# Three quarters of a load on half of the DMA engines: two tilted 512 KB loads and an earlier loop on VectorE

## The chip, the cores and the metric

The kernel runs on one core of a Trainium2 chip. The metric is the device time of one execution in microseconds (us); of several runs the median is given. A core has a matrix engine (TensorE, PE in the profile; PEld is its weight load), VectorE (DVE), ScalarE (ACT), GpSimd (POOL) and SyncE (SP). SP issues all the loads here, and sixteen DMA engines carry them from HBM to SBUF.

## The reference

Two layers of one decode step: four tokens (B = 4, one position each, D = 512), each layer a grouped-query attention over a cache of 8192 positions and a gated feed-forward block. Both layers use the same weights and the same caches.

```
B, D, Hq, Hkv, Sk, Dh, F = 4, 512, 32, 8, 8192, 128, 1792        # bf16
def attention(x):
    q = (x @ wq).reshape(B, 1, Hq, Dh) transposed to heads
    scores = q . k_cache * Dh**-0.5          # each of 8 cache heads serves 4 query heads
    o = softmax(scores) @ v_cache
    return o.reshape(B, 1, Hq * Dh) @ wo
def ffn(x): return (silu(x @ w_gate) * (x @ w_up)) @ w_down
for layer in (1, 2):
    x = x + attention(layernorm(x))
    x = x + ffn(layernorm(x))
```

k_cache and v_cache are [4, 8, 8192, 128], so each is 64 MB. They have to be read once per layer, apart from what is kept on the chip between the layers.

## The kernel before

**Units.** A unit is one pair of token and cache head: 32 per layer. Its K tile and its V tile are 2 MB each, 128 partitions by 16 KB. SBUF has eight slots for such tiles (`kvf`, seen as `kv`), and the weights of the feed-forward block lie in two of the slots while they are needed. Three units of layer 1 stay in SBUF and are used first in layer 2.

**The order of the loads** is one list, `items`: K and V tiles of the units, the four pieces of `wo` (1 MB each, two DMAs of 512 KB) among the first of them, and `w_gate`, `w_up` and `w_down` at the end of a layer. `pump()` walks this list while the program is built and issues the next load when its slot is free; on the chip SP waits on semaphores for the engines that used the slot before. A load is described by `runs()`: 512 KB become 32 rows of 16 KB in HBM against 128 partitions by 4 KB in SBUF, and 2 MB become 64 rows of 32 KB. Some units are loaded in quarters of 512 KB (`part`); among them is the first K tile of layer 2 that isn't kept. Its first three quarters are issued in `ffn` of layer 1, after the products with `w_gate`, as `part(ks[0], NKEEP, 0, w6, sem_p[0])`, since they go to where `w_gate` lay.

**The work of a unit.** VectorE transposes the K tile in eight pieces (`turn`), TensorE multiplies them by the query (`scores`), VectorE takes the maximum, ScalarE the exponentials, VectorE transposes the probabilities (`turn_p`), TensorE multiplies them by V, and VectorE adds the parts up (`own_others`). After every fourth unit all four tokens of a cache head are done, and `out_proj` multiplies by a slice of `wo`: TensorE spreads the result, VectorE copies it to `o4` (that copy waits until all of `wo` is there), TensorE multiplies. Every TensorE, VectorE and ScalarE operation is recorded on a tape first, with the waits that it needs.

**The repeated blocks.** `roll()` plays the tape of each engine. It looks for the longest stretch of a layer in which four units (`CYCLE`) do the same as the next four, with the same semaphores in the waits, and emits that stretch as a loop; what lies ahead of it, between the layers and behind it is emitted unrolled. A wait inside the loop is on a value computed in a register, as the counts rise by a fixed step per turn. On VectorE the first `out_proj` has four waits more than the others (one for each piece of `wo`), so the loop of layer 1 starts at unit 7 of 32 and turns six times. TensorE's loop of layer 1, which has no such difference, starts at unit 3 and turns seven times.

**The semaphores.** A DMA raises its semaphore by 16 when it is complete, and the trace shows these increments one by one, as each DMA engine finishes its share. The four pieces of `wo` have a semaphore each.

In the profile nearly all operations of TensorE stand under line 99, those of VectorE and ScalarE under line 117, and the loads under line 135, as helpers emit them; waits of SP stand under line 79. The loops are at lines 885 to 891.

Of the kernel before, what the change touches and what calls it, by code (L numbers as in the profile page):

```python
# [27 lines left out]
class _Sync:  # L28
# [81 lines left out]
            if sig:  # L110
                ins.then_inc(self.prog[engname], 1)

    def op(self, engname, fn, reads=(), writes=(), sig=True):
        left = self._open(engname, self._need(reads, writes))
        if engname in self.LATE:
            name, args, kw = fn(_Call())
            self.tape[engname].append((repr((name, args, kw)), lambda e, _: getattr(e, name)(*args, **kw), left, sig, None))  # L117
        else:
            for sem, val in left:
                self.eng[engname].wait_ge(sem, val)  # L120
            ins = fn(self.eng[engname])
            if sig:
                ins.then_inc(self.prog[engname], 1)
        self.count[engname] += sig
        self._record(engname, (self.prog[engname], self.count[engname] + (not sig)), reads, writes)
# [20 lines left out]
def bass_interleave_layers__gqa_block_cached__swiglu_ffn__decode_kernel(  # L146
# [18 lines left out]
    P = 128  # L165
    assert Dh == P and B * Hq == P and D % P == 0 and F % P == 0 and B == 4
    KT = D // P
    FO = F // P
# [12 lines left out]
    NKEEP = 6  # L181
# [9 lines left out]
    with ExitStack() as es:  # L191
# [9 lines left out]
        kv = kvf[:, 0:NSLOT * SL].rearrange("p (s w) -> p s w", s=NSLOT)  # L201
# [15 lines left out]
        wo_sb = sb("wo_sb", [P, G, REP, D], BF16)  # L217
# [9 lines left out]
        o4 = sb("o4", [P, REP, B], BF16)  # L227
# [8 lines left out]
        pb = sb("pb", [P, SW], BF16)  # L236
# [8 lines left out]
        n = 2 * FO * B  # L245
# [13 lines left out]
        def few(ap):  # L259
# [6 lines left out]
        STEP, TOT, OUTB, LNB = 4, 5, 6, 7  # L266
# [7 lines left out]
        sem_p = [sem(f"sem_p{i}") for i in range(6)]  # L274
        sem_x = sem("sem_x")
        sem_w = {n: [sem(f"sem_{n}{i}") for i in range(c)]
                 for n, c in (("wq", KT), ("wo", 4), ("wg", KT), ("wu", KT), ("wd", FO // 2))}
        sem_out = sem("sem_out")
        es.enter_context(nc.Block())
        T = _Sync(nc, engines, prog)  # L280
# [6 lines left out]
             reads=["ident"], writes=["ident"])  # L287
        T.op("pool", lambda e: e.memset(quad[:], 0.0), writes=["quad"])
        for a in range(NA):
# [8 lines left out]
             reads=["ident"], writes=["head"])  # L298
        T.op("dve", lambda e: e.tensor_reduce(acc[:, 0:QB], identf[:].rearrange("p (y h) -> p y h", h=REP), AX.X, ALU.max),
             reads=["ident"], writes=["acc"])  # L300
        T.op("dve", lambda e: e.tensor_reduce(own[:], acc[:, 0:QB].rearrange("p (a y) -> p y a", a=NA)[:, 0:NV, :],
                                              AX.X, ALU.max),
             reads=["acc"], writes=["own"])
# [26 lines left out]
        for L in range(2):  # L330
            seq = [it for it in work(L) if it not in kept]
            for k, v in ((29, 27), (30, 28)):

                it = ("K", L, unit_order[L][k])
# [26 lines left out]
        def runs(src):  # L361

            n = src.shape[0] * src.shape[1] * 2
            return src.rearrange("(r k) n -> r (k n)", r=32 * -(-n // (32 * RUN)))

        def load_weight(name, i=0):
            if name == "wq":
                T.dma("sp", [(wq_sb[:, i, :], runs(A_wq[i * P:(i + 1) * P, :]))], sem_w["wq"][i], writes=[f"wq{i}"])
            elif name == "wo":
                n = G // 4  # L370
                w = REP * Dh
                T.dma("sp", [(wo_sb[:, g, :, :].rearrange("p e n -> p (e n)"), runs(A_wo[g * w:(g + 1) * w, :]))
                             for g in range(i * n, (i + 1) * n)], sem_w["wo"][i], writes=[f"wo{i}"])
            elif name == "wg":
                for k in range(KT):
                    T.dma("sp", [(wg_sb[:, k, :], runs(B_w_gate[k * P:(k + 1) * P, :]))], sem_w["wg"][k],
                          writes=(places if k == 0 else []) + [f"wg{k}"])
            elif name == "wu":
                for k in range(KT):
                    T.dma("sp", [(wu_sb[k], runs(B_w_up[k * P:(k + 1) * P, :]))], sem_w["wu"][k], writes=[f"wu{k}"])  # L380
            else:
                for j in range(FO // 2):
                    T.dma("sp", [(wd_sb[:, 2 * j:2 * j + 2, :].rearrange("p e n -> p (e n)"),
                                  runs(B_w_down[2 * j * P:(2 * j + 2) * P, :]))], sem_w["wd"][j], writes=[f"wd{j}"])
# [29 lines left out]
                    T.dma("sp", [(kv[:, s, :], runs(cache[b, g, :, :]))], sem_s[s], writes=[f"s{s}.{q}" for q in range(NB)])  # L414
                issued[0] += 1

        def part(it, s, a, b, sem_):
            kind, L, u = it
            assert (L, u) in fours
            n = NB // NQ  # L420
            w, m = n * TB * Dh, S // NQ
            src = (A_k_cache if kind == "K" else A_v_cache)[u % B, u // B, :, :]
            T.dma("sp", [(kv[:, s, q * w:(q + 1) * w], runs(src[q * m:(q + 1) * m, :])) for q in range(a // n, b // n)],
                  sem_, writes=[f"s{s}.{k}" for k in range(a, b)])

        def place(it, s):
# [261 lines left out]
        def out_proj(g, more):  # L688

            pick = ident.rearrange("p (j e) -> p e j", e=REP)  # L690
            ob = bank(OUTB)[:, XB:2 * XB].rearrange("p (e b) -> p e b", b=B)
            warm(*((3, TOT) if more else (2,)))
            for c in range(REP):
                for h in range(REP):
                    T.pe(ob[h * QB:(h + 1) * QB, c, :], pick[:, c, :], oT[:, g // (G - 1), h, :],
                         reads=[f"oT{g // (G - 1)}", "ident"], writes=[f"pb{OUTB}"], sig=(h == REP - 1),
                         start=True, stop=True)
            T.op("dve", lambda e: e.tensor_copy(o4[:], ob),
                 reads=[f"pb{OUTB}"] + [f"wo{i}" for i in range(4)], writes=["o4"])
            warm(*((5, TOT) if more else (2,)))  # L700
            for nt in range(KT):
                for c in range(REP):
                    T.pe(bank(OUTB)[:, nt * B:nt * B + WIDE], ((c, nt), wo_at(c * D + nt * P)), few(o4[:, c, :]), at=g,
                         reads=["o4"], writes=[f"pb{OUTB}"], sig=(c == REP - 1), start=(c == 0), stop=(c == REP - 1))
# [78 lines left out]
        def ffn(last):  # L783
# [8 lines left out]
            for (w_sb, wname, bk) in (([wg_sb[:, k, :] for k in range(KT)], "wg", gb), (wu_sb, "wu", ub)):  # L792
                out = bank(bk)[:, 0:WIDE // B * FO * B].rearrange("p (r f b) -> p f r b", f=FO, b=B)
                for kt in range(KT):
                    if bk == gb and kt == KT // 2:
                        deviation(zero_sb, "zero")
                    if bk == ub and kt and not last:
                        warm(3)
                    for fo in range(FO):
                        f = fo // 2 * 2 * P + fo % 2  # L800
                        w = up3(f) if bk == ub and kt == FR and last else w_sb[kt][:, f:f + 2 * P - 1:2]
                        T.pe(out[:, fo, :, :], w, few(xn[:, kt * B:(kt + 1) * B]),
                             start=(kt + fo == 0), stop=(kt == KT - 1 and fo == FO - 1),
                             reads=["up3"] if bk == ub and kt == FR and last else at_w[wname] + [f"{wname}{kt}", "xn"],
                             writes=[f"pb{bk}"],
                             sig=(fo == FO - 1 and kt == KT - 1))
                if bk == gb and not last:
                    place(ks[0], NKEEP)
                    part(ks[0], NKEEP, 0, w6, sem_p[0])
            T.op("dve", lambda e: e.tensor_tensor(fb(gr), fb(gT), rb, ALU.mult),  # L810
                 reads=[f"pb{gb}", "rstd"], writes=["gr"])
            T.op("act", lambda e: e.activation(eg, gr, ACTF.Exp, scale=-1.0), reads=["gr"], writes=["eg"])
# [36 lines left out]
        def roll(name):  # L849
# [18 lines left out]
            for L in range(2):  # L868
                run = {}
                for n in range(L * NU + 1, L * NU + NU - CYCLE - 1):  # L870
                    m = n
                    while m + CYCLE < L * NU + NU - 1 and said[m] == said[m + CYCLE] and strides(m) and \
                            strides(m) == strides(n + (m - n) % CYCLE):
                        m += 1
                    run[n] = m - n
                n = max(run, key=run.get)
                turns = run[n] // CYCLE + 1
                assert turns >= 3
                step = {}
                for k in range(n, n + CYCLE):  # L880
                    for key, d in strides(k).items():
                        assert step.setdefault(key, d) == d
                assert step.get(None, 1) == 1
                T.play(name, ops[at:heads[name][n]])
                with nc.Fori(1, 1 + turns, 1, engines=(only,), head_slot={only: HEADS[L]} if name == "pe" else None) as i:  # L885
                    for k in range(n, n + CYCLE):
                        value = {}
                        for _, _, left, _, _ in part[k]:
                            for sem_, v in left:
                                d = step[id(sem_)]  # L890
                                value[id(sem_), v] = engine.to_reg(i * d + (v - d))  # L891
                        T.play(name, part[k], lambda sem_, v: value[id(sem_), v], lambda g: i + (g - 1))
                at = heads[name][n + CYCLE * turns]
            T.play(name, ops[at:])
# [73 lines left out]
```

## Time and profile before

| What | Value |
|---|---|
| median of 3 runs | 644.71 us (644.68 to 647.39) |
| profiled execution | 645.19 us, its span 643.4 us |
| bytes read from HBM | 273.42 MB, 425 GB/s over the span |
| busy share of the span | PE 80%, PEld 52%, DVE 70%, ACT 19%, POOL 3% |
| DMA queue of the loads | 99.1% of sixteen engines' span |
| 512 KB loads of wo | 8, median 38.0 us from issue to landing |
| 512 KB loads of K | 20, median 9.0 us from issue to landing |
| chain of waits that ended last | DMA 63%, PE 19%, DVE 13%, SP's queue 2%, issue 1%, ACT 1% |
| granted TensorE clock | 0.902 of full speed |

The span runs from the first to the last instruction of the profiled execution; its own time holds about 1.8 us more. Queue q1 carries the loads that SP issues. q8 and q14 are packets of the kind "instruction", with which the engines fetch their programs; they run on the same sixteen DMA engines. A busy share is an average over the whole span; the chain of waits names, step by step back from the end, what each piece of work was released by.

### The profile page before, as it was taken

To read this page: it belongs to the slowest core of one execution; us is meant where nothing else is said; L and a number is where in the kernel's file an instruction comes from. 1 tells how busy PE (TensorE), PEld (TensorE's weight loads), DVE (VectorE), ACT (ScalarE), POOL (GpSimd) and SP (SyncE) were. 2 spreads that over 40 slices of the span, in tenths; PEclk is the share of its full clock that TensorE was granted. 3 is DMA by queue.
4 is the path that set the end of the run, shared out by engine and by line. 5 is a ranking of instruction groups with operands and counts; after the bars stand their busy time and mean duration, and the time that the engine had idled before them with its cause. 6 is when DMAs were issued, how large, how long until landed. Compare 5 with 4: busy or idle time off the path is not lost.

```text
span 643.4 us, 13044 instructions
## 1 busy us (share of the span) xinstructions
PE 515.1 (80%) x5064; PEld 332.7 (52%) x5087; DVE 448.5 (70%) x1104; ACT 119.6 (19%) x396; POOL 19.3 (3%) x73
## 2 busy tenths in 40 slices
PE   1656888887879788787888898898987769788888
PEld 1434555554545555454555565565554445465555
DVE  2646676776876867868763749989686686686783
ACT  0111121211211212211221312212121121121221
POOL 0000000000000000000000000000000000000000
PEclk9967697789896977999999979999889887987898
DMA  8999999999999999999999999999999999999996
GB/s 359 441 435 419 428 441 438 424 430 440 430 428 434 436 430 428 441 434 428 426 425 419 417 444 420 431 439 430 426 436 442 424 434 430 440 424 434 428 429 280
DMA packets 12744, 273.76 MB, mean 425 GB/s; under 512 B 3048, under 2 KB 3056, under 8 KB 3056
## 3 DMA queue, kind: packets, MB, share of 16 engines
q1 hardware_dynamic: 12720, 273.44, 99.1%
q8 instruction: 16, 0.26, 0.2%
q14 instruction: 8, 0.07, 0.0%
HBM read 273.42 MB, written 0.00 MB: 425 GB/s over the span
## 4 chain that ended last, share of the span: by engine, by line
DMA 63%; PE 19%; DVE 13%; SPq 2%; issue 1%; ACT 1%; DVEq 0%; POOL 0%; POOLq 0%
DMA kvf<-in_A_k_cache_dram 49%; PE ps L99 19%; DMA kvf<-in_A_v_cache_dram 12%; DVE kvf L117 9%; DMA kvf<-in_B_w_down_dram 2%; SPq L135 2%; DVE acc L117 2%; DVE one L117 1%; DVE m L117 0%; DVE pT L117 0%; ACT pb L117 0%; ACT acc L117 0%; DVE oT L117 0%; DVEq L891 0%; DVEq L885 0%
## 5 line engine op out<-in xcount | busy, mean ns | idle before, releaser
L117 DVE STREAM_TRANSPOSE kvf<-kvf 128x512 f32<-128x512 f32 x488 | 322.5, 686 | 89.5 <-DMA kvf<-in_A_k_cache_dram 89.5
L99 PE MATMUL ps<-kvf,zq 128*128 128x256 bf16 x2048 | 314.7, 296 | 16.4 <-DVE kvf L117 9.0
L99 PEld LDWEIGHTS ps<-kvf,zq 128*128 128x128 bf16 x2048 | 196.2, 107 | 78.6 <-DVE kvf L117 29.4
L117 ACT ACTIVATE pb<-m 1x128 f32<-1x128 f32 x64 | 19.7, 308 | 433.9 <-DVE m L117 433.7
L99 PE MATMUL ps<-kvf,pT 128*16 128x512 bf16 x992 | 67.7, 395 | 12.3 <-DVE rl L117 8.2
L117 DVE SCALAR_TENSOR_TENSOR acc<-ps,own,acc 128x128 f32<-128x128 f32 x186 | 65.2, 350 | 5.4 <-ACT acc L117 0.7
L99 PE MATMUL ps<-identf,one 128*1 128x128 f32 x64 | 17.7, 277 | 48.2 <-DVE one L117 48.1
L99 PEld LDWEIGHTS ps<-identf,one 128*1 128x1 f32 x64 | 5.1, 80 | 77.0 <-DVE one L117 73.1
L99 PEld LDWEIGHTS ps<-kvf,pT 128*16 128x16 bf16 x992 | 19.4, 89 | 42.2 <-issue 23.9
L117 ACT ACTIVATE pb<-ps,one,rstd 128x256 bf16<-128x256 f32 x64 | 36.0, 563 | 2.1
L99 PE MATMUL ps<-head,acc 128*128 128x4 f32 x124 | 23.7, 262 | 15.6 <-DVE acc L117 15.6
L99 PEld LDWEIGHTS ps<-head,acc 128*128 128x128 f32 x124 | 21.4, 216 | 28.3 <-DVE acc L117 26.7
L487 POOL TENSOR_TENSOR zq<-scr,quad 128x64 bf16<-128x64 bf16 x62 | 18.1, 292 | 599.6 <-PE ps L99 448.7
L117 DVE TENSOR_REDUCE one<-ps 128x1 f32<-128x256 f32 x64 | 26.0, 406 | 13.7 <-PE ps L99 13.5
L99 PEld LDWEIGHTS ps<-one,pb 1*128 1x128 f32 x128 | 21.3, 207 | 27.0 <-ACT pb L117 23.2
L117 DVE RECIPROCAL rl<-ps 128x4 f32<-128x4 f32 x64 | 10.4, 162 | 34.4 <-PE ps L99 34.4
L99 PE MATMUL ps<-one,pb 1*128 1x1 f32 x128 | 26.8, 276 | 9.4 <-ACT pb L117 9.3
L99 PE MATMUL ps<-wq_sb 128*128 128x512 bf16 (+1 forms) x92 | 28.5, 377 | 1.9 <-issue 1.1
L117 DVE STREAM_TRANSPOSE pT<-pb 128x256 bf16<-128x256 bf16 x64 | 26.1, 407 | 4.6 <-ACT pb L117 4.5
L99 PEld LDWEIGHTS ps<-o,wo_sb 128*128 (+1 forms) x256 | 20.5, 100 | 8.5 <-issue 4.4
L99 PE MATMUL ps<-o,wo_sb 128*128 128x32 bf16 x256 | 24.4, 181 | 0.3
L99 PE MATMUL ps<-xn,wq_sb 128*128 128x32 bf16 x270 | 19.4, 182 | 5.6 <-DMA wq_sb<-in_A_wq_dram 4.9
(65 smaller groups left out, 245.0 us busy)
## 6 DMA issues: line engine op xcount, KB each, us to landing
kvf<-in_A_k_cache_dram SPq DMA_DIRECT2D x56, 2048.0 KB, 29.1
kvf<-in_A_v_cache_dram SPq DMA_DIRECT2D x56, 2048.0 KB, 32.6
kvf<-in_A_k_cache_dram SPq DMA_DIRECT2D x20, 512.0 KB, 9.0
kvf<-in_A_v_cache_dram SPq DMA_DIRECT2D x20, 512.0 KB, 11.9
wq_sb<-in_A_wq_dram SPq DMA_DIRECT2D x4, 1024.0 KB, 7.4
wo_sb<-in_A_wo_dram SPq DMA_DIRECT2D x8, 512.0 KB, 38.0
kvf<-in_B_w_gate_dram SPq DMA_DIRECT2D x8, 448.0 KB, 18.1
kvf<-in_B_w_down_dram SPq DMA_DIRECT2D x14, 256.0 KB, 18.7
```

The costliest lines, as they stand in the source:

```text
L99: return e.matmul(out, lhsT=lhsT if at is None else lhsT(place(at)), rhs=rhs, **kw)
L117: self.tape[engname].append((repr((name, args, kw)), lambda e, _: getattr(e, name)(*args, **kw), left, sig, None))
L135: ins = e.add_instruction(mybir.InstDMACopy(name=self.nc.get_next_instruction_name(), mode="Copy", queue="qSPDynamicHW", ins=e.lower_ap_dm ...
L487: T.op(eng, lambda e: e.tensor_tensor(dst, q4, m4_, ALU.mult), reads=keys_ + ["quad"], writes=["zq"])
```

## The change

Two loads are tilted. `tilted` replaces one 512 KB DMA by two: the first half of the source goes as 16 rows of 16 KB to partitions 0 to 63, and the second half as 8 rows of 32 KB to partitions 64 to 127. A DMA of 16 rows is spread over sixteen DMA engines and one of 8 rows over eight, so that the lower eight engines carry 48 KB each and the upper eight 16 KB each, instead of 32 KB each. The two loads are the first 512 KB of `wo`, near the start, and the first quarter of the first K tile of layer 2 that isn't kept (`ks[0]`), issued in `ffn` of layer 1.

The four pieces of `wo` now share one semaphore, and the wait for `wo` is no longer a read of four resources that only the first `out_proj` has to wait for. It is a wait that every `out_proj` carries (`hold`), always on the same constant value, the count after the last piece. All units of layer 1 then look alike to `roll` from unit 3 on, and VectorE's loop of that layer can start at unit 3 and turn seven times. A wait whose value doesn't change per turn is emitted on the constant itself.

```
     def op(self, engname, fn, reads=(), writes=(), sig=True, hold=()):
         left = self._open(engname, self._need(reads, writes)) + list(hold)
...
-                 for n, c in (("wq", KT), ("wo", 4), ("wg", KT), ("wu", KT), ("wd", FO // 2))}
+                 for n, c in (("wq", KT), ("wo", 1), ("wg", KT), ("wu", KT), ("wd", FO // 2))}
...
+        def whole(to, src):
+            return [(to, runs(src))]
+
+        def tilted(to, src):
+
+            n = src.shape[0] // 2
+            return [(to[k * P // 2:(k + 1) * P // 2, :],
+                     src[k * n:(k + 1) * n, :].rearrange("(r k) n -> r (k n)", r=r)) for k, r in enumerate((16, 8))]
...
-                T.dma("sp", [(wo_sb[:, g, :, :].rearrange("p e n -> p (e n)"), runs(A_wo[g * w:(g + 1) * w, :]))
-                             for g in range(i * n, (i + 1) * n)], sem_w["wo"][i], writes=[f"wo{i}"])
+                T.dma("sp", [p for g in range(i * n, (i + 1) * n)
+                             for p in (tilted if g == 0 else whole)(wo_sb[:, g, :, :].rearrange("p e n -> p (e n)"),
+                                                                    A_wo[g * w:(g + 1) * w, :])],
+                      sem_w["wo"][0], writes=[f"wo{i}"])
...
-        def part(it, s, a, b, sem_):
+        def part(it, s, a, b, sem_, tilt=()):
...
-            T.dma("sp", [(kv[:, s, q * w:(q + 1) * w], runs(src[q * m:(q + 1) * m, :])) for q in range(a // n, b // n)],
+            T.dma("sp", [p for q in range(a // n, b // n)
+                         for p in (tilted if q in tilt else whole)(kv[:, s, q * w:(q + 1) * w], src[q * m:(q + 1) * m, :])],
                   sem_, writes=[f"s{s}.{k}" for k in range(a, b)])
...
-                 reads=[f"pb{OUTB}"] + [f"wo{i}" for i in range(4)], writes=["o4"])
+                 reads=[f"pb{OUTB}"], writes=["o4"], hold=[T.res["wo3"].w])
...
-                    part(ks[0], NKEEP, 0, w6, sem_p[0])
+                    part(ks[0], NKEEP, 0, w6, sem_p[0], tilt=(0,))
...
-                                value[id(sem_), v] = engine.to_reg(i * d + (v - d))
+                                value[id(sem_), v] = engine.to_reg(i * d + (v - d)) if d else v
```

More of the change, by code (lines that the diff above doesn't have):

```diff
@@ L111, in play, with op @@
                 ins.then_inc(self.prog[engname], 1)
-    def op(self, engname, fn, reads=(), writes=(), sig=True):
-        left = self._open(engname, self._need(reads, writes))
+    def op(self, engname, fn, reads=(), writes=(), sig=True, hold=()):
+        left = self._open(engname, self._need(reads, writes)) + list(hold)
         if engname in self.LATE:
```

## The prediction, made before the changed kernel was run

> **What bounds the kernel now.** I read the page's DMA part first, then the busy time by stage, then the chain of waits near the end, then the waits of SP and VectorE.
>
> The page's DMA part gives queue, packets, MB and share of sixteen engines' span:
>
> ```profile
> DMA packets 12744, 273.76 MB, mean 425 GB/s; under 512 B 3048, under 2 KB 3056, under 8 KB 3056
> ...
> q1 hardware_dynamic: 12720, 273.44, 99.1%
> q8 instruction: 16, 0.26, 0.2%
> q14 instruction: 8, 0.07, 0.0%
> ```
>
> The loads' queue is busy for 99.1% of the span, so sixteen DMA engines that never rest set the time. Stage by stage it is the same (the last two columns are DMA share and GB/s):
>
> ```profile
> 25.00:72.00 47.00, 30.77 (x250) 19.66 (x247) 25.15 (x59) 6.83 (x23) 1.17 (x4) 0.75 0.99 422
> 72.00:112.00 40.00, 33.12 (x288) 21.70 (x289) 28.55 (x69) 7.08 (x24) 1.17 (x4) 0.83 1.00 432
> 370.00:440.00 70.00, 63.54 (x660) 42.26 (x662) 55.24 (x139) 14.59 (x50) 2.63 (x9) 0.95 1.01 432
> ```
>
> The chain of waits from 600 us (start, length, what) shows what the end hangs on:
>
> ```profile
> 614.80 17.07 DMA kvf<-in_A_v_cache_dram
> ...
> 631.91 0.79 PE ps L99 x17
> ...
> 634.34 6.99 PE ps L99 x156
> 641.33 0.02 issue
> 641.35 0.42 DVE scr L117
> ```
>
> The last V quarter lands at 631.86, and 9.5 us of dependent work follow. The time is therefore that landing plus a fixed tail, and the landing is the slowest engine's: a load is there when all sixteen have delivered. They are not level, as the DMA share in 0.55 us slices from 622 to 644 us shows:
>
> ```profile
> DMA  9697949999999999999999989997664200000000
> ```
>
> From 636 us the share falls in steps (7, 6, 6, 4, 2) instead of breaking off: engines run out of work one after another. The trace has each load's sixteen completion counts, one per engine. For the last V quarter they come at 628.53 for the first engine, with four others within 0.25, four 0.85 to 1.0 behind it, five at 2.36 to 2.51, one at 2.65 and one at 3.33; for the last w_down load it is nearly the same list with the slowest at 3.26. There the average engine is 1.5 behind the first, so perfect levelling could win 3.26 - 1.5 = 1.8 us, 0.27%. That is all there is to win here.
>
> **Where the lag comes from.** All engines move 32 KB in 1.215 us and 16 KB in 0.615 us throughout; what sets them apart are the packets of q8 and q14. Each of the sixteen q8 packets (16 KB, about 1.0 us, and the next data packet 0.5 us longer) puts one engine 1.5 us back; each of the eight q14 packets (8 KB, 0.31 us, next packet up to 0.6 longer) puts one up to 0.91 us back. Following the engines by their lags, the q8 packets go round the same eight engines twice. The q14 packets at 41.35, 118.07, 388.30 and 629.27 us all hit one engine, call it A, and its last one makes it the slowest (2.35 + 0.91 = 3.26).
>
> **The VectorE part.** Its program is 489 instructions of 64 bytes: 122 before the first loop, passes of 80, 138 between the loops, 55 after. At A's four packets VectorE has executed 50, 189, 722 and 1249 instructions; with loop passes taken out these are places 50, 189, 322 and 449 of the program, 128 apart and later, which is 8 KB. So A's packets are VectorE's code. The change drops the four waits on wo from the first out_proj and gives each out_proj the same one, so the first loop can start at the third unit instead of the seventh: four unrolled units, about 70 instructions, leave the front and the program ends near 410 to 415. Place 449 no longer exists, so the packet at 629 us goes: **-0.91 us on engine A**, 3.26 to 2.35.
>
> The moved code itself costs nothing on the path. One more pass is one more turn of the loop, whose branches show as 0.06 and 0.07 us in the chain of waits, and the units concerned run where VectorE waits for data (wait, total us, times, longest):
>
> ```profile
> DVE kvf L117 <- DMA kvf<-in_A_k_cache_dram: 16.5, 3, 8.2
> ```
>
> That is 30 to 70 us. If that cover were gone, the turn would cost 0.13 us. The new wait sits in front of the cast of o4, first at 79.77 us; the last wo load lands at 66.4. Queued behind it are the K transposes, and TensorE waits for those, but a wait that is 13 us late never holds.
>
> **The tilt.** A normal 512 KB load gives every engine two 16 KB packets. A tilted one gives sixteen 16 KB packets (first half of the partitions) and eight 32 KB packets (second half): 48 KB on each lower engine, 16 KB on each upper one. Per load the lower eight gain one 16 KB packet and the upper eight lose one, 0.615 us each way; two loads make **+1.23 us on the lower eight, -1.23 us on the upper eight**, if a packet costs what it costs elsewhere. Both loads are issued while everything is saturated (5.67 and 340.38 us), so the shift stays to the end. Each adds one issue of 0.6 us on SP. At 5.67 nine issues follow and then SP waits until 24.25; at 340.38 two follow, ahead of a wait that ends at 345.12:
>
> ```profile
> SPq L79 <- PE ps L99: 498.1, 110, 19.4
> ```
>
> SP waits 498 us in all, so the two issues are covered; uncovered they would be 1.2 us. The tilted loads themselves are wanted late (wo at 79.8; VectorE has no wait for K between 340 and 440 us).
>
> Which engines are the lower ones? The trace does not name them. In the very first load eight engines start at 2.08 to 2.15 us and the other eight at 2.73 to 2.78, and the four packets of x (four rows) run on engines of the first eight, so I take the first eight as the lower ones. [...] By their lag at 27 us (four engines of the first eight are 0.3 us back, no other is) A is one of the first eight. Of the eight that q8 hits, seven fit the second eight; one, hit at 330 us and now 2.65 back, is again one of those four.
>
> **The sum** at the end, behind today's first engine: A 3.26 - 0.91 + 1.23 = 3.58; the 2.65 engine 2.65 + 1.23 = 3.88; the other lower ones at most 2.2; the upper ones 2.5 - 1.23 = 1.3. The slowest goes from 3.26 to 3.88: **+0.6 us**. The profiled execution took 645.19 us (span 643.40 plus 1.79 around it), 0.48 above the median of the runs, 644.71; the difference applies to both, so 645.8 profiled and 645.3 as median.
>
> The unknown price is a packet that writes where other engines write; no load of before does that. The nearest row is the 512 KB load with each engine in its own rows, 0.615 us a packet, extra 0. The upper bound is full sharing. The first piece puts sixteen engines on half the partitions: 0.615 more for all. In the second the lower eight write 32 KB where the upper eight are writing: 1.215 more for all. That is 1.83 per load and 3.66 for both. A gain is excluded, as no packet is shorter. I take 0: nothing in the trace shows one engine slowed by another, and after each instruction packet only the hit engine is late. [...]
>
> **Rivals.**
> 1. *Level* (faster, within 0.5%). If A and the 2.65 engine are upper ones after all, the q8 set is exactly the upper eight: upper 2.65 - 1.23 = 1.4, lower 0.95 + 1.23 = 2.2, A 1.1. The slowest goes from 3.26 to 2.2: -1.1 us, 643.6. For it: seven of eight fit. Against: the 0.3 us group.
> 2. *Crowding* (slower). The half loads share a way into the partitions: +3.66 + 0.6 = +4.3 us, 649.0; with only the second pieces colliding +3.0, 647.7; and if the 32 KB packets, which span eight partitions where normal ones span four at most, also collide among themselves, 2.4 more: 651.4. It decides once a 16 KB packet of the first piece takes over 0.9 us. For it: packets run at one speed everywhere, as if at a limit. Against: no slowed neighbour.
> 3. *No tilt*. If the eight-row piece does not go to the lower eight, only the VectorE part is left: slowest 2.65, -0.6 us, 644.1.
>
> **How the numbers follow.** A measurement of this kernel can tell 0.5%, 3.2 us, from no change (the three runs spread 2.7). Forecast 0.40, level 0.27, crowding 0.27 (two thirds of it over 3.2 us), no tilt 0.06. Slower by over 0.5%: 0.18 from crowding and 0.02 from scatter. Faster by over 0.5%: no case reaches it; 0.04 for scatter. Range: from level less 0.3 to full crowding, 643.3 to 649.0; outside lie some scatter and the worst crowding.
>
> **What would show it.** q14 has seven packets, none near 629 us. Each tilted load leaves eight 32 KB and sixteen 16 KB packets; their durations (0.615 and 1.215, or up to double) decide rival 2. The counts of the last V quarter: slowest 3.9 behind today's first engine by the forecast, all within 1.1 of each other by *level*. The forecast is wrong if the last V quarter lands before 631.9 or after 633, or if the chain's tail is no longer 9.5 us.

## The result, and the profile after

The changed kernel takes 650.21 us (median of 5 runs, 649.84 to 651.21) against 645.15 us for the kernel before beside it (644.68 to 647.39). The ratio is 1.0075, with a 95% interval of 1.0061 to 1.009. The prediction was 645.3 us, range 643.3 to 649.0. The profiled execution took 651.21 us, 1.0 above its median, with a span of 649.3.

The DMA part of the page of after:

```profile
DMA packets 12743, 273.76 MB, mean 422 GB/s; under 512 B 3064, under 2 KB 3072, under 8 KB 3072
...
q1 hardware_dynamic: 12720, 273.44, 99.0%
q8 instruction: 16, 0.26, 0.2%
q14 instruction: 7, 0.06, 0.0%
```

q14 has seven packets; they lie at 48, 177, 273, 340, 350, 403 and 419 us, none near 629. The DMA engines are as occupied as before (99.0%), yet move 422 GB/s instead of 425. So no engine is idle for longer; packets take longer. The busy time by stage says where (the last two columns are DMA share and GB/s; a packet counts whole where it starts, so a share can exceed 1 and the rate of a short row is coarse):

```profile
25.00:72.00 47.00, 30.04 (x240) 19.97 (x239) 26.60 (x61) 6.84 (x23) 1.17 (x4) 0.76 1.02 415
72.00:112.00 40.00, 33.23 (x291) 21.19 (x290) 28.27 (x67) 7.09 (x24) 1.17 (x4) 0.85 1.00 432
370.00:440.00 70.00, 62.28 (x642) 41.42 (x644) 54.46 (x137) 16.40 (x56) 2.64 (x9) 0.98 1.01 431
```

The later two stages are as they were. The first, which holds the tilted load of wo, fell from 422 to 415 GB/s with its DMA share at 1.02. Cut closer around the two tilted loads, first the kernel before, then the changed one:

```profile
26.00:34.00 8.00, 3.41 (x28) 2.37 (x25) 2.33 (x5) 1.52 (x5) 0.29 (x1) 0.88 1.03 440
344.00:356.00 12.00, 11.02 (x152) 6.90 (x154) 4.28 (x15) 2.35 (x4) 0.29 (x1) 1.00 1.03 426
```

```profile
26.00:34.00 8.00, 5.25 (x44) 3.81 (x41) 3.78 (x8) 1.52 (x5) 0.58 (x2) 1.00 1.05 334
344.00:356.00 12.00, 8.39 (x134) 4.74 (x138) 2.10 (x11) 0.12 (x1) 0.00 (x0) 0.90 1.02 315
```

Engines as fully occupied as before move 334 and 315 GB/s instead of 440 and 426. That is what engines in each other's way would show; the experiments below test it. The second place in slices of 0.5 us from 344 to 364 us:

```profile
GB/s 406 393 340 471 373 442 426 410 344 229 344 508 246 180 410 213 246 98 164 229 197 262 295 328 426 295 492 426 393 459 262 393 426 229 492 459 393 295 262 393
```

From the ninth slice (348 us) to the twenty-fourth (356) fourteen of sixteen stay below 350. The packets of the trace say the same: around the wo load the eight 32 KB packets of the tilt, all under way at once from 28.13 to 29.31 us and so on eight engines, take 1.9 to 2.6 us instead of 1.215, and 16 KB packets of other loads beside them 1.26 to 1.34 instead of 0.615; around the K quarter the 32 KB packets take 1.81 to 2.58.

What arrives late stays late. The last V quarter lands at 638.09 (631.86 before), its first engine 3.39 ahead; the last w_down load at 646.79 (640.51 before). The end of the chain of waits (start, length, what):

```profile
629.39 17.40 DMA kvf<-in_B_w_down_dram
646.79 0.04 issue
646.84 0.43 PE ps L99 x4
647.29 0.42 DVE scr L117
```

and the DMA share in 0.55 us slices from 628 to 650 us:

```profile
DMA  8979978999999999999999989998563100000000
```

The chain now reaches the end through the last w_down load rather than through the last V quarter and its 9.5 us tail. The two are about level: 638.09 + 9.5 would be 647.6, and the last step starts at 647.3. What follows the landings is as before, shifted by some 6 us in this execution. SP still waits 500 us in all, so its two additional issues are covered as assumed, and VectorE's wait for K between 30 and 70 us is 17.3 us, 0.8 more than before:

```profile
SPq L79 <- PE ps L99: 499.7, 109, 17.0
```

```profile
DVE kvf L117 <- DMA kvf<-in_A_k_cache_dram: 17.3, 3, 9.0
```

### The profile page after: what moved, and what is told of

It reads as the page before. It is cut to its first block, busy times and chain, and to the rows that moved or that the text cites. A ratio compares the mean times of both kernels' runs of the same rounds, so it can differ in the third digit from the quotient of the medians.

```text
span 649.3 us, 13064 instructions
## 1 busy us (share of the span) xinstructions
PE 523.7 (81%) x5064; PEld 338.8 (52%) x5087; DVE 448.9 (69%) x1104; ACT 119.7 (18%) x396; POOL 19.3 (3%) x73
## 4 chain that ended last, share of the span: by engine, by line
DMA 65%; PE 16%; DVE 11%; SPq 5%; issue 1%; ACT 1%; DVEq 0%; POOL 0%; POOLq 0%
DMA kvf<-in_A_k_cache_dram 52%; PE ps L99 16%; DMA kvf<-in_A_v_cache_dram 8%; DVE kvf L117 7%; DMA kvf<-in_B_w_down_dram 5%; SPq L135 5%; DVE acc L117 2%; DVE one L117 1%; DVE m L117 0%; DVE pT L117 0%; ACT pb L117 0%; DVE oT L117 0%; ACT acc L117 0%; DVEq L903 0%; POOL zq L499 0%
## 5 line engine op out<-in xcount | busy, mean ns | idle before, releaser
L99 PE MATMUL ps<-kvf,zq 128*128 128x256 bf16 x2048 | 321.9, 301 | 15.6 <-DVE kvf L117 12.0
L99 PEld LDWEIGHTS ps<-kvf,zq 128*128 128x128 bf16 x2048 | 200.9, 109 | 78.6 <-DVE kvf L117 25.2
L99 PEld LDWEIGHTS ps<-rsm,one 128*128 128x128 f32 x128 | 22.3, 217 | 4.0 <-ACT rsm L117 2.5
```

Of the source, the lines that this page charges most:

```text
L99: return e.matmul(out, lhsT=lhsT if at is None else lhsT(place(at)), rhs=rhs, **kw)
```

## Experiments

Each kernel is an edit of the changed one, timed beside the kernel before (645.1 to 645.3 us in all of them). "Late" below is how much later, on average over the sixteen completion counts, a load is than in the kernel of the VectorE part alone, in the profiled executions: first the K load that lands near 72 us, behind the wo place; then the last w_down load, behind both places. An average over engines shows what was lost to slower packets; a mere shift of bytes from upper to lower engines leaves it where it is.

| Kernel | Median us | Ratio to before, 95% | Late near 72 us | Late at the end |
|---|---|---|---|---|
| changed kernel | 650.21 | 1.0061 to 1.009 | 2.22 | 5.84 |
| VectorE part alone | 644.42 | 0.9982 to 0.9999 | 0 | 0 |
| + wo tilted | 647.26 | 1.002 to 1.0046 | 1.91 | 1.99 |
| + first K quarter tilted | 646.99 | 1.0024 to 1.005 | 0.07 | 1.89 |
| + third K quarter tilted | 647.19 | 1.0019 to 1.0042 | 0.14 | 2.24 |
| halves, both 16 rows | 647.46 | 1.0033 to 1.0073 | 0.87 | 1.83 |
| even and odd partitions, tilted | 649.07 | 1.0049 to 1.0075 | 2.08 | 3.83 |
| even and odd, both 16 rows | 646.95 | 1.0017 to 1.0037 | 0.89 | 1.99 |
| halves exchanged, tilted | 648.98 | 1.0054 to 1.0097 | 1.70 | 3.75 |
| whole height, 16 rows of 32 KB | 648.23 | 1.003 to 1.0069 | 1.29 | 2.68 |
| four pieces of 8 rows | 649.92 | 1.006 to 1.0086 | 1.10 | 3.65 |
| three pieces, eight rows in 0 to 63 | 647.55 | 1.0025 to 1.0051 | 0.49 | 1.78 |
| three pieces, halves exchanged | 648.98 | 1.0043 to 1.007 | 0.81 | 3.12 |

### Which part costs the time

**VectorE part alone.** Both loads whole; the rest of the change stays.

```
-  for p in (tilted if g == 0 else whole)(wo_sb[:, g, :, :]...
+  for p in whole(wo_sb[:, g, :, :]...
...
-  part(ks[0], NKEEP, 0, w6, sem_p[0], tilt=(0,))
+  part(ks[0], NKEEP, 0, w6, sem_p[0])
```

> VectorE part alone: both loads go whole, one semaphore and the wait in every out_proj stay. Crowding (the 5 us of the changed kernel are the tilted loads slowing each other's writes): the slowest engine at the end is 2.65 behind the first instead of 3.26, so 0.6 us below the kernel before, about 644.5, and the last w_down count at about 639.9 us. Rival, the loop (the longer loop of VectorE or the wait in every out_proj costs the time): 2 us or more above the kernel before, and the two tilted loads give the rest. Rival, bytes (lower engines end later only because they carry more): also 0.6 us below, but then the next two kernels lie within 1 us of this one.

644.42 us, 0.8 below the kernel before beside it; the last w_down count comes at 639.96. Longer loop and moved wait cost nothing that shows, and q14 has seven packets here too. The rival of a costly loop falls. With both tilted loads gone, the two places run at about the rates of the kernel before (440 and 426 GB/s):

```profile
26.00:34.00 8.00, 4.56 (x37) 3.45 (x37) 3.35 (x7) 1.52 (x5) 0.37 (x2) 1.00 1.07 457
344.00:356.00 12.00, 10.91 (x150) 6.72 (x147) 4.24 (x15) 2.35 (x4) 0.29 (x1) 1.00 1.02 423
```

**Only wo tilted** (the first K quarter whole) and **only the first K quarter tilted** (wo whole).

> VectorE part, and only the load of wo tilted. Crowding by place: the trace of the changed kernel shows every engine about 1.8 us later after this load, and the lower engines 0.6 more; so about 2 us above the kernel of the VectorE part alone, 646.5, and every packet between 36 and 340 us as before. Rival, bytes: +0.6 us over the VectorE part alone, about 645.1, first engine not later. Rival, one lump (the 5 us come from the second tilt alone, the first is made good again): the same as the VectorE part alone within 0.3 us.

> VectorE part, and only the quarter of K tilted. Crowding with an amplifier of its own at this place (engines 3.3 us apart, w_down ahead in the queue, TensorE waiting for it): about 4.4 us above the VectorE part alone, some 648.9, the eight 32 KB packets at 1.8 to 2.6 us each and other loads' packets slowed for 8 us. Rival, full sharing and no amplifier: 1.83 + 0.6 above, about 646.9. Rival, the second is dear only because the first has set the engines apart: about 1.8 to 2.5 above, and the packets slowed for under 6 us.

647.26 and 646.99: 2.84 and 2.57 us above the VectorE part alone, where about 2 and 4.4 were expected. The sum, 644.42 + 2.84 + 2.57 = 649.8, is the changed kernel within 0.4. Neither the bytes alone nor one lump does it; each tilted load costs by itself, and where it stands. The first line is from the kernel with wo tilted, the second from the one with the K quarter tilted:

```profile
26.00:34.00 8.00, 4.35 (x37) 3.22 (x34) 2.92 (x6) 1.52 (x5) 0.29 (x1) 1.00 1.02 334
```

```profile
344.00:356.00 12.00, 10.65 (x147) 6.49 (x143) 3.17 (x13) 2.35 (x4) 0.00 (x0) 1.00 1.02 351
```

Against 457, 334 GB/s over 8 us are 0.98 MB that were not moved, some 2.3 us of loading at 422 GB/s; the counts say 1.91. An amplifier at the K quarter, which I had read out of the changed kernel's trace (4.4 us there), doesn't show: alone it costs 2.57. With K alone the last w_down load is 1.36 us later for its first engine and 2.59 for its last. Full sharing (1.83) minus and plus one 16 KB packet (0.615) is 1.22 and 2.45.

**The third K quarter instead of the first** (`tilt=(2,)`, wo whole), so that w_down doesn't stand just ahead.

> VectorE part, and of the K tile the third quarter is tilted instead of the first; wo is whole. The price at the first quarter alone was 2.6 us. If a tilt costs full sharing wherever all engines are busy (1.83 and the shift of 0.6): again 2.4 to 2.6 above the VectorE part alone, 646.9. Rival, place (part of the price arises because w_down stands just ahead, for which TensorE waits): under 1.5 above, 645.5, since the last w_down count is then not later than without a tilt.

647.19, 2.77 above the VectorE part alone. Behind other quarters the price is the same within the scatter, so TensorE's wait for w_down is not the cause.

### What of a tilted load is slow

**Two halves without a tilt.** `enumerate((16, 16))` in place of `enumerate((16, 8))`: every engine carries 32 KB again, in two DMAs of 64 partitions.

> Both loads in two pieces of 64 partitions, but with sixteen rows of 16 KB each, so that every engine carries 32 KB as in a whole load. Half-partition crowding (any piece that writes only half the partitions goes at half speed): both pieces cost 0.6 us for all engines, 1.2 per load, about 2.5 us above the VectorE part alone, 647. Rival, neighbours (only lower engines writing into the upper engines' half collide, that is the eight-row piece): under 0.7 us per load, 645. Rival, rows (only the 32 KB row across eight partitions is slow): 16 KB packets at 0.615 us as ever, same time as the VectorE part alone.

647.46. Rows of 16 KB, evenly spread, are slow too, 0.61 to 1.05 us a packet; by the medians about half of the price (3.0 of 5.8 us) is there without the eight-row piece:

```profile
26.00:34.00 8.00, 3.74 (x32) 2.70 (x29) 2.52 (x5) 1.52 (x5) 0.29 (x1) 0.92 1.01 387
```

This spoke for half the partitions being the cause. The next three runs were to confirm it.

**Pieces on even and odd partitions**, with the tilt and without it:

```
-  return [(to[k * P // 2:(k + 1) * P // 2, :],
+  return [(to[k:P:2, :],
...
-  ... for k, r in enumerate((16, 8))]
+  ... for k, r in enumerate((16, 16))]      # second kernel only
```

> Both loads tilted as in the changed kernel, but the sixteen-row piece goes to the even partitions and the eight-row piece to the odd ones, so each piece writes over the whole height. Rows of the source land in other partitions than the products assume, so the output isn't the reference's; bytes, rows and DMA engines stay. Half-partition crowding: packets at 0.615 and 1.215 us as in whole loads, so only the tilt of the bytes is left and the time is 643.6 to 645.5. Rival, two pieces or eight rows as such: as the changed kernel, 650, 32 KB packets at 2 us and more. Rival, wide rows (a packet that reaches over more partitions is slower): 16 KB packets over 0.7 us and 651 or more.

> As the pieces on even and odd partitions, but both with sixteen rows of 16 KB, so without a tilt; again rows land in other partitions and the output isn't the reference's. Half-partition crowding: 16 KB packets at 0.615 us, the same time as the VectorE part alone, 644.4, against 647.5 with the pieces on halves. Rival, two DMAs instead of one: 647 as with the halves.

649.07 and 646.95, where 643.6 to 645.5 and 644.4 were expected. The pieces reach over the whole height and are about as slow as on halves; "half the partitions" falls as the cause. The rate at the wo place, first with the tilt, then without:

```profile
26.00:34.00 8.00, 4.87 (x40) 3.47 (x38) 3.72 (x7) 1.52 (x5) 0.58 (x2) 1.00 1.09 358
```

```profile
26.00:34.00 8.00, 3.83 (x32) 2.77 (x30) 2.59 (x6) 1.52 (x5) 0.29 (x1) 0.93 1.00 383
```

**Halves exchanged**: `enumerate((8, 16))`.

> Both loads tilted, with the halves exchanged: the eight-row piece goes first and to partitions 0 to 63, the sixteen-row piece to 64 to 127. Half-partition crowding: it doesn't matter which half, 649.5 to 650.5. Rival, neighbours (collision only where the lower engines write beside the upper engines' rows): the eight-row piece no longer collides, so under 1 us per load is left, about 646.5.

648.98, 0.5 below the expected interval and far above the rival's 646.5. The rival as I had put it falls: with the eight-row piece in partitions 0 to 63 the price over the VectorE part alone is still 4.56 us, and the wo place runs at 358 GB/s. The rows of that piece are 32 KB, eight partitions each.

### Who slows whom: rows, pieces and places

The fast loads have one shape: a whole 512 KB load has rows of four partitions over the full height, and its 16 KB packets take 0.61 us. Every other cut so far cost time over the VectorE part alone, for both loads: 3.04 us with sixteen rows on each half, 4.56 and 5.79 us with a tilt on halves. Rows of 16 KB on even partitions also span eight, and the spread over the whole height won little (646.95 against 647.46). The following four runs, expected ahead, vary width, cut and place. What was expected of them rests on two estimates of mine: which engines write into the same place, and that packets which meet there take twice as long, 0.615 us more for 16 KB and 1.23 for two of them. No run shows either as such. The trace names neither the engine nor the partitions of a packet, so the kernels are judged by packet times and totals.

**Whole height, one DMA, sixteen rows of 32 KB.** No cut and no tilt; only the width of a row changes.

```
+  n, m = src.shape[0] // P, P // 4
+  return [(to[a * m:b * m, :], src[a * m * n:b * m * n, :].rearrange("(r k) n -> r (k n)", r=r))
+          for a, b, r in ((0, 4, 16),)]
```

> Both loads whole again, one DMA each over all 128 partitions, 32 KB per engine and no tilt; only the rows differ: sixteen of 32 KB (eight partitions each) instead of thirty-two of 16 KB (four partitions each). [...] Rival, pieces (a load cut in two DMAs, or pieces over half the height, is what costs): no cut here, so 1.215 us a packet and 644.4, as the VectorE part alone.

648.23: slow without any cut, and the rival (pieces) falls. The time is 1.4 above 646.8, my estimate with 1.2 us a load, with runs from 646.9 to 651.9. The sixteen 32 KB packets take 1.70 to 2.00 us instead of 1.21 and the 16 KB packets behind them up to 1.07; the load near 72 us is 1.29 late.

```profile
26.00:34.00 8.00, 4.73 (x39) 3.45 (x37) 3.72 (x7) 1.52 (x5) 0.58 (x2) 1.00 1.05 391
```

**Four pieces of 32 partitions, eight rows of 16 KB each**: `((0, 1, 8), (1, 2, 8), (2, 3, 8), (3, 4, 8))`.

> Both loads as four pieces of 32 partitions, eight rows of 16 KB each, all on the eight lower engines: 64 KB on a lower engine and none on an upper one, twice the tilt of the change, and no row wider than four partitions. [...] Upper engines -1.23 + 1.23, lower engines +1.23 + 1.23 per load: the slowest about 4.9 later for two loads, 649.3, less if the lower engines were not the late ones. Rival, pieces (few partitions or few rows are slow as such): all four packets slow, over 1 us from the first on, and 652 or more.

649.92, 0.6 above what was expected. The packets of the wo place, in the order in which they start:

| From us | Eight engines, the four pieces | Other eight engines, later loads |
|---|---|---|
| 27.3 | 16 KB, 0.61 us | 16 KB, 0.61 |
| 27.9 | 16 KB, 0.61 | 16 KB, 0.61 |
| 28.5 | 16 KB, 0.62 to 0.77 | 32 KB, 1.82 to 1.97 (alone 1.21) |
| 29.2 | 16 KB, 1.21 | the same packets |

Two pieces at full speed and two that are slowed together with the other side; rows and piece sizes are the same in all four. A half of the partitions is not slow in itself: the same eight engines, by the starts above, write 16 KB in 0.61 us into one half and in up to 1.21 us into the other. One rival was not tried: no kernel changes only where a piece is read from, so engines that meet at HBM are not excluded by a run of their own. Against that rival speak these four pieces, which are read in the same way, eight rows of 16 KB each, and of which only the last two are slow. For it speaks that pieces on even and odd partitions, read just as on halves, cost about as much (649.07 against 650.21 us with the tilt, 646.95 against 647.46 without).

**Three pieces**: `((0, 1, 8), (1, 2, 8), (2, 4, 16))`, and **the same with the halves exchanged**: `((2, 3, 8), (3, 4, 8), (0, 2, 16))`.

> Both loads tilted by as much as in the changed kernel (48 KB on a lower engine, 16 KB on an upper one), but in three pieces: partitions 0 to 31 and 32 to 63 by eight rows of 16 KB each, 64 to 127 by sixteen rows of 16 KB. [...] Per load everything 0.6 later and the lower engines another 0.6: 646.0 to 646.9, below the kernel with exchanged halves (648.98), which differs in nothing but the width of the rows. Rival, pieces: three pieces cost more than two, 650 or more.

> As the three pieces before (tilt as in the changed kernel, all rows 16 KB and four partitions wide), with the halves exchanged: the two eight-row pieces go to partitions 64 to 95 and 96 to 127, the sixteen-row piece to 0 to 63. [...] Rival, shape (how many pieces, rows and partitions decides, not which): 647.5, packets at 0.61 as there.

The first takes 647.55, 0.65 above the interval but 2.7 below the changed kernel with the same tilt, and 1.4 below the kernel with exchanged halves (648.98), which puts its eight rows into the same half but makes them twice as wide: the eight-row packets run at 0.61 us, and 0.49 of the reckoned 0.6 is lost per engine at the wo place. The exchanged one of three pieces also takes 648.98, 1.4 more with nothing changed but the place. My estimate was 2.5 more, 650.0, with packets slowed from the first on; the direction is right, the size not: the first packets run at 0.61 there too, and only from the second on do both sides take 0.76 to 1.06. Why the first ones are spared was not shown.

```profile
26.00:34.00 8.00, 4.22 (x36) 3.12 (x33) 2.79 (x6) 1.52 (x5) 0.29 (x1) 0.99 1.05 424
```

```profile
26.00:34.00 8.00, 5.16 (x43) 3.72 (x40) 3.88 (x8) 1.52 (x5) 0.58 (x2) 1.00 1.05 412
```

Together: in the kernel of four pieces, eight rows of 16 KB took 0.61 us a packet in partitions 0 to 63 and 0.62 to 1.21 in 64 to 127, and wide rows took 1.70 to 2.00 us instead of 1.21. The load of sixteen wide rows goes to all 128 partitions and cost 1.29 us all the same, so full height alone is not enough here; the whole loads that ran at 0.61 have rows of at most four partitions as well.

## Why the prediction was wrong, step by step

- **The bound and the end**: right. DMA engines set the time, and landings 6.2 us later in the profiled execution made a span 5.9 longer. The tail stayed, within 0.3 us.
- **The VectorE part, -0.91 us on one engine, -0.6 in all**: right. The packet at 629 us is gone, the part alone measured 0.76 below the kernel before, and its slowest engine ends 2.61 behind its first (3.26 before, 2.65 reckoned). The reading of the program was off without harm: the parts listed add up to 475 instructions, not 489, and the packets' places are 139, 133 and 127 apart, not 128; for the 8 KB of a packet that is 59 to 65 bytes an instruction. Cover for SP's issues and the new wait: right.
- **The tilt, 0.615 us down for the upper engines and up for the lower**: right as far as it shows. With the K quarter alone, first and last engine part by 1.23 more than without.
- **The failed step: "The unknown price is a packet that writes where other engines write ... I take 0."** It is not 0 but about the upper bound: 1.83 reckoned per load, 1.91 and 1.89 measured on the average engine. The argument for 0 was that nothing in the trace shows one engine slowed by another. That trace could not show it: all its large loads have rows of at most four partitions over the full height, and their packets take 1.21 us for 32 KB and 0.61 for 16 KB. The row that spoke against it was on the table, packets at one speed everywhere "as if at a limit"; the 0.27 that I gave it was too low.
- **The bounds given to it were of the right size**: rival 2's sum, 649.0, was 1.2 too low, and its worst case, in which the wide packets also meet among themselves (651.4), too high. The wide packets have a price of their own: in partitions 0 to 63, narrow rows in their place gave 1.4 us back with the tilt unchanged (648.98 to 647.55), and sixteen wide rows alone cost 1.29 a load. That 1.83 fits so well is therefore in part luck: it is an estimate that no run shows as such; narrow rows cost less than reckoned (0.87 of 1.23 a load in two sixteen-row pieces, 0.49 of 0.6 in the three pieces), and the wide packets' own price, which 1.83 leaves out, made up for it. "It decides once a 16 KB packet of the first piece takes over 0.9 us" was the wrong mark; those of the first piece took 0.61 to 0.79, and the delay came out in the packets behind them.
- **Open**: single tilts cost 2.6 to 2.8 us by their medians, 2.45 by the sum of sharing and bytes; and the profiled execution of the changed kernel lost 5.8 on the average engine where the two single ones lost 3.9. One us of that is this execution's distance above its median, and 0.6 is that of the kernel with wo tilted, which was profiled 0.6 below its own. By the medians, both loads together cost 0.4 more than the sum of the two alone, and for that no cause was tested. At the second place the engines stand 2 to 4 us apart (2.1 in the kernel before, 3.6 in the changed one), so which packets run at the same time may differ from run to run.
- **Rival 1, *Level***: did not come. No tilted kernel here came below the VectorE part alone (644.42 us); the lowest has the first K quarter tilted, 646.99. Whether a tilt whose packets slow no others would have brought it, no run shows.

Of all kernels run, the VectorE part alone is the best, 644.42 us.

## What to carry to other kernels

Cut a load as the loads that ran at full speed are cut: full height, rows of at most four partitions here; all other cuts cost 1.3 to 2.9 us a load by the medians. Before shifting bytes between engines, time one load in the new shape: packets that never vary (1.21 and 0.61 us in the kernel before) can be a sign of a limit, and a trace in which all loads have one shape says nothing of another shape (up to 2.58 us for 32 KB in the changed kernel). A DMA share near 1 at a lower GB/s is how the collision looked in these profiles (1.02 at 315 GB/s, against 1.03 at 426).

## What was not expected of the hardware

- A single 512 KB DMA over all 128 partitions loses about 1.3 us (1.29 at the wo place) if its rows are 32 KB (eight partitions) instead of 16 KB (four), with equal bytes per engine.
- The delay lands partly on the next packet: in the three pieces the 16 KB packets that were slowed first took 0.61 to 0.79 us, those right behind them 0.90 to 1.01.
- The loss is the same within the scatter whether w_down or other K quarters stand ahead in the queue (2.57 and 2.77 us).
